# Attention, soft mixture of experts and a feed-forward layer in one kernel: the first slice of the folded feed-forward weight is made in two halves, six subtractions move from GpSimd to VectorE, and decode steps of ScalarE are placed behind the activations of their unit

## The chip, the cores and the metric

The kernel runs on one core of one Trainium2 chip. Its time is the device time of that core in microseconds (us). The engines work side by side, each through its own queue of instructions in order, and wait for one another through semaphores: TensorE (PE in the profile, with its weight loads as PEld), VectorE (DVE), ScalarE (ACT), GpSimd (POOL) and SyncE (SP), which only issues DMAs here.

## What is computed

```python
# attention: q, k, v (4, 8, 576, 64), window of 128, linear bias, softmax
scores = where(mask, q @ k.T / 8 + slope * -|i - j|, -1e9)
x = softmax(scores) @ v                        # -> (2304, 512)
# soft mixture of experts: 8 experts with 4 slots each
logits = x @ phi                               # (2304, 32)
slot_in = softmax(logits, axis=0).T @ x        # (32, 512)
slot_out[e] = relu(slot_in[e] @ w1[e]) @ w2[e] # (32, 512)
y = softmax(logits, axis=1) @ slot_out         # (2304, 512)
# feed-forward layer, d_ff = 2048
h = y @ w_in                                   # (2304, 2048)
out = maximum(0.01 * h, h) @ w_out             # (2304, 512)
```

`w_in` and `w_out` come as float64; the kernel reads each value as two 32-bit words and builds a float32 from them.

## The kernel before

The work runs in three stages: attention with the router's logits (to about 150 us), the experts (to about 210 us), and the feed-forward layer. The change lies in the last one.

**Folding.** `y @ w_in` is computed as `c @ (slot_out @ w_in)`, where `c` holds the combine weights. `M = slot_out @ w_in` has only 32 rows, so that the first layer is one matmul of 128 x 128 by 128 x 384 for each unit (`stage1`, L951). The operand of M is `mst`: its rows hold M's rounded high part and, on partitions 64 to 127, the remainder. `emit_M` (L918) makes M for one chunk or two of 256 columns in two parts. Part 0: four matmuls of `soT` (the slot outputs transposed) with the decoded `w_in` chunk, one for each 128 of the 512 rows, side by side on TensorE (L923), and a copy by ScalarE (L926). Part 1: a matmul with the constant `blk` that sums them (L928), a rounding copy by ScalarE into `mst` (L930), and a subtraction by VectorE that leaves the remainder (L931). `soT` comes from `to_soT` (L808): four transposes on TensorE and four copies by VectorE of 32 columns each (L814).

**Units.** The 2304 rows are taken in blocks of 384 (`TB`), the 2048 hidden columns in 16 groups of 128 (f). A unit is one block with one f; `visits` lists the 96 units in the order of work. For a unit, `stage1` puts the first layer into a PSUM tile `ph` (two buffers), `round_g` (ScalarE, L955) writes the activation rounded for TensorE, `full_g` (ScalarE, L959) the full one, `rest_g` (VectorE, L963) their difference, and `emit_o` (L965) adds nine matmuls of 512 columns (L973) into three PSUM accumulators: rounded activation by the rounded weight (WO1), by the weight's remainder (WO2), and remainder by the rounded weight. After the last f of a visit, `finish` moves the accumulators to a spill buffer, adds them to it, or writes the output; ScalarE does two of each three copies, VectorE one (L988).

**Decoding.** The weights come in eight chunks of `w_in` and eight of `w_out`, each 1 MB. `decode` (L733) turns one into float32 in two halves: a step on ScalarE for each half (`sq`, an Abs with a scale), three on VectorE (`ops`, a shift and two logical combinations), and for `w_out` a rounding copy by ScalarE into WO1 and a subtraction that leaves WO2 (`tail`, L771 and L772). All have line L757 in the profile. In chunk 0 the subtraction is VectorE's, in the others GpSimd's.

**The order** is a table of numbers: `at_(y, f)` enters a step at place y, in units, and the steps are issued sorted by y (L1057). `stage1` of unit n has y = n, its activations n + 0.121 and n + 0.174, its second layer n + 1.9 rising to n + 3.986. ScalarE's decode steps stand at y - 0.33 of their chunk's entry in `DEC`, M of later chunks at `MY`, and the transposes of the last batch of combine weights (`ctr`, L851) at 16.3 and 17.1. `keep` issues matmuls on constants that fill waits of TensorE; `WX` gives how many. SP issues the loads of later chunks in the order of `loads`.

Of the kernel before, what the change touches and what calls it, by code (L numbers as in the profile page):

```python
# [21 lines left out]
def attn_softmoe_ffn(ctx: ExitStack, tc: tile.TileContext, q, k, v, phi, w1, w2, w_in, w_out, cst_in, out):  # L22
    nc = tc.nc
# [96 lines left out]
    with tc.manual_schedule():  # L120
# [578 lines left out]
        FPC = NF // NCH  # L699
        fw = DFF // NCH  # L700
        TB = 384
        WX = {"i": 1, "s": 1, "t": 2, "m": 2, "b": 3, "h": 3}
        x0 = off["x0"]

        def parts(w, *os):
# [27 lines left out]
        def decode(c, split):  # L733
# [22 lines left out]
            def op(l, f, *a, **kw):  # L756
                l.append(lambda: f(*a, **kw))  # L757
# [9 lines left out]
            if split:  # L767
                for i, d in enumerate(dd):
                    w1v = WO1[c].rearrange("p a b -> p (a b)")[:, n * i:n * i + n]
                    w2v = WO2[c].rearrange("p a b -> p (a b)")[:, n * i:n * i + n]  # L770
                    op(tail, nc.scalar.copy, out=w1v, in_=d)  # L771
                    op(tail, (nc.gpsimd if c else nc.vector).tensor_tensor, out=w2v, in0=d, in1=w1v.bitcast(F32), op=ALU.subtract)  # L772
            return sq, ops, tail

        bctx = ExitStack()
# [142 lines left out]
        def emit_M(cs, part):  # L918
# [8 lines left out]
            else:  # L927
# [78 lines left out]
        def at_(y, f, *a):  # L1006
            ev.append((y, len(ev), lambda: f(*a)))

        for n, u in enumerate(units):
            o = n + min(1.9 + .13 * n, ZO["O"])  # L1010
            at_(n, stage1, *u)
            at_(n + ZO["T"], round_g, *u)
            at_(n + ZO["H"], full_g, *u)
            at_(n + ZO["V"], rest_g, *u)
            at_(o, emit_o, *u)
            if u[2] == visits[u[0]][3] - 1:
                for i in range(3):
# [89 lines left out]
```

## Time and profile before

| | |
|---|---|
| median of 3 runs | 451.87 us (450.97 to 452.1) |
| the profiled execution | 450.6 us, of which the span is 448.9 us |
| TensorE busy | 432.3 us (96%) |
| VectorE busy | 283.8 us (63%) |
| ScalarE busy | 240.7 us (54%) |
| GpSimd busy | 128.3 us (29%) |

The span runs from the first to the last instruction on the core; the profiled execution's own time has 1.7 us around it. It is 1.3 us below the median. The shares are means over stages with different limits, and a busy TensorE is not one at its peak, since its records overlap; so the stage in question is read from the timeline.

### The profile page before, as it was taken

How to read it: one execution, taken by the hardware profiler on the slowest of the kernel's cores; microseconds unless marked ns; L12 is line 12 of the kernel's file. 1: busy time of each engine (PE TensorE's matmuls, PEld its weight loads, DVE VectorE, ACT ScalarE, POOL GpSimd, SP SyncE). 2: the span in 40 equal slices, each digit the busy share in tenths (PEclk: the TensorE clock that was granted, in tenths of full speed). 3: DMA queues.
4: the chain of work that ended last, by engine and by line, in shares of the span. 5: the costliest groups of instructions: out<-in, count | busy, mean ns of one | idle time of the engine just before them, and what ended most of it. 6: DMA issues, size and time to landing. Idle time of an engine off the chain costs nothing.

```text
span 448.9 us, 9854 instructions
## 1 busy us (share of the span) xinstructions
PE 432.3 (96%) x3498; PEld 340.3 (76%) x3498; DVE 283.8 (63%) x887; ACT 240.7 (54%) x555; POOL 128.3 (29%) x302
## 2 busy tenths in 40 slices
PE   8899999999999999999998999999999999999996
PEld 7788888888888785334775788878878888888885
DVE  5999889999999945022798767675562223225242
ACT  4586777577677641021784865555545335333330
POOL 3477567576567743020010222020202000000000
PEclk9999999999999999999999999999999999999999
DMA  8389889889888878999966150000000003003011
GB/s 169 103 229 238 224 244 243 215 240 246 216 226 241 250 219 300 343 386 395 397 239 234 45 154 34 1 1 1 1 0 0 1 0 142 0 0 142 1 72 70
DMA packets 66834, 70.30 MB, mean 157 GB/s; under 512 B 23169, under 2 KB 42017, under 8 KB 66785
## 3 DMA queue, kind: packets, MB, share of 16 engines
q1 hardware_dynamic: 66640, 69.53, 50.7%
q8 instruction: 28, 0.46, 0.5%
q14 instruction: 22, 0.17, 0.1%
q10 hardware_dynamic: 144, 0.13, 0.1%
HBM read 64.85 MB, written 4.72 MB: 155 GB/s over the span
## 4 chain that ended last, share of the span: by engine, by line
PE 76%; DVE 9%; DMA 7%; ACT 5%; issue 2%; SPq 0%; POOL 0%; DVEq 0%; ACTq 0%; POOLq 0%
PE acc L973 41%; PE o_ps L407 4%; DMA qb<-ms 4%; PE ph L951 3%; PE pb L822 3%; PE st L343 3%; PE sm L301 3%; PE st L342 3%; DMA ar<-in_moe_w_out_dram 3%; PE tp L261 2%; PE o_ps L151 2%; DVE junk L311 2%; PE tp L449 1%; DVE kq L279 1%; PE pb L875 1%
## 5 line engine op out<-in xcount | busy, mean ns | idle before, releaser
L973 PE MATMUL acc<-p,p 128*128 128x512 f32 x648 | 161.1, 393 | 0.0
L973 PEld LDWEIGHTS acc<-p,p 128*128 128x128 f32 x648 | 120.4, 188 | 27.0 <-issue 2.6
L963 DVE TENSOR_TENSOR p<-ar,p 128x384 fp32r<-128x384 f32 x96 | 56.5, 598 | 98.2 <-ACT ar L959 98.1
L955 ACT ACTIVATE p<-ph 128x384 fp32r<-128x384 f32 x96 | 47.4, 493 | 96.2 <-PE ph L951 96.2
L973 PE MATMUL acc<-b,p 128*128 128x512 f32 x216 | 55.5, 400 | 1.3 <-DVE p L963 1.3
L311 DVE CUSTOM_DVE_ANT_0 junk<-sm,ar 128x256 bf16<-128x256 f32 (+2 forms) x160 | 53.5, 375 | 4.2 <-PE sm L301 4.0
L350 ACT ACTIVATE ar<-st 128x512 f32<-128x512 f32 x64 | 38.3, 599 | 19.3 <-PE st L343 10.2
L973 PEld LDWEIGHTS acc<-b,p 128*128 128x128 f32 x216 | 40.0, 188 | 10.8 <-DVE p L963 1.7
L959 ACT ACTIVATE ar<-ph 128x384 f32<-128x384 f32 x96 | 46.9, 488 | 0.0
L757 POOL TENSOR_TENSOR p<-ar,p 128x512 fp32r<-128x512 f32 x12 | 15.9, 1322 | 90.5 <-ACT p L757 58.8
L342 PE MATMUL st<-kq 128*128 128x256 f32 (+1 forms) x160 | 40.1, 278 | 0.0
L407 PE MATMUL o_ps<-ar 128*64 128x65 f32 x992 | 39.0, 225 | 0.0
L301 PE MATMUL sm<-kb,qb 96*128 96x256 f32 (+2 forms) x160 | 34.9, 312 | 3.4 <-ACT kb L274 1.4
L407 PEld LDWEIGHTS o_ps<-ar 128*64 128x64 f32 x992 | 34.8, 138 | 4.1 <-issue 1.5
L343 PE MATMUL st<-qb,kb 128*128 128x256 f32 (+1 forms) x160 | 36.2, 273 | 1.6 <-DMA qb<-ms 1.5
L951 PE MATMUL ph<-p,p 128*128 128x384 f32 x96 | 32.0, 338 | 0.7 <-DVE p L931 0.4
L274 ACT ACTIVATE qb<-tp 64x288 fp32r<-64x288 f32 x64 | 27.7, 433 | 9.1 <-PE tp L261 7.9
L279 DVE SCALAR_TENSOR_TENSOR kq<-tp,qb 64x288 fp32r<-64x288 f32 x64 | 29.2, 457 | 4.3 <-ACT qb L274 2.2
L287 POOL TENSOR_SCALAR_AFFINE_SELECT kq<-qb 64x576 fp32r<-64x576 f32 x32 | 21.1, 661 | 37.2 <-ACT qb L274 29.6
L274 ACT ACTIVATE kb<-tp 64x288 fp32r<-64x288 f32 x64 | 27.9, 437 | 6.0 <-PE tp L261 4.6
L343 PEld LDWEIGHTS st<-qb,kb 128*128 128x128 f32 (+1 forms) x160 | 28.6, 179 | 2.9 <-DMA qb<-ms 2.8
L281 DVE TENSOR_TENSOR kq<-tp,kb 64x288 fp32r<-64x288 f32 x64 | 29.1, 455 | 1.7
(190 smaller groups left out, 615.5 us busy)
## 6 DMA issues: line engine op xcount, KB each, us to landing
p<-in_moe_w_dram SPq DMA_DIRECT2D x56, 256.0 KB, 4.4
p<-in_moe_w_dram SPq DMA_DIRECT2D x7, 1024.0 KB, 11.6
p<-in_moe_w_in_dram SPq DMA_DIRECT2D x5, 1024.0 KB, 5.5
p<-in_moe_w_out_dram SPq DMA_DIRECT2D x5, 1024.0 KB, 15.4
ar<-in_k_dram SPq DMA_DIRECT2D x32, 144.0 KB, 4.0
ar<-in_q_dram SPq DMA_DIRECT2D x32, 144.0 KB, 3.7
out_dram<-ar SPq DMA_DIRECT2D x17, 256.0 KB, 2.2
ar<-in_v_dram SPq DMA_DIRECT2D x32, 128.0 KB, 3.9
```

Source lines behind the costliest of these rows:

```text
L274: nc.scalar.activation(out=b1, in_=pr, func=AF.Copy, scale=2.0 ** (g % H - 2) if half else 1.0)
L301: nc.tensor.matmul(sl, lhsT=Q1[0:MROW, 128 * t:128 * t + mr], rhs=K1[0:MROW, c0:c1], start=True, stop=True)
L311: nc.vector.tensor_tensor_reduce(out=jk[0:mr, 0:n], in0=sl, in1=maskt[0:mr, m0:m0 + n], op0=ALU.add, op1=ALU.max, accum_out=mn[g % 2][0:mr ...
L342: nc.tensor.matmul(sl, lhsT=KX[:, k0:k1], rhs=QA[:, q0:q1], start=True, stop=False)
L343: nc.tensor.matmul(sl, lhsT=kb[g % R][:, k0:k1], rhs=qb[g % R][:, q0:q1], start=False, stop=True)
L350: nc.scalar.activation(out=e, in_=sts.pop((g, s)), func=AF.Exp, scale=2.0 ** -(g % H + 1))
L407: nc.tensor.matmul(o_ps[64 * u:64 * u + 64, t, :], lhsT=lt, rhs=r, start=st, stop=sp, tile_position=(0, 64 * u))
L951: nc.tensor.matmul(p, lhsT=mst[:, 128 * f:128 * f + 128], rhs=rhs, start=True, stop=True)
L955: nc.scalar.activation(out=G[t0, f][0], in_=H1[t0, f], func=AF.Prelu, alpha=0.01)
L959: nc.scalar.activation(out=gg, in_=H1.pop((t0, f)), func=AF.Prelu, alpha=0.01)
L963: nc.vector.tensor_tensor(out=g2, in0=G0.pop((t0, f)), in1=g1.bitcast(F32), op=ALU.subtract)
L973: nc.tensor.matmul(acc[t0][t], lhsT=(g1, g1, g2)[k][:, 128 * t:128 * t + 128], rhs=(WO1, WO2, WO1)[k][c][:, i], start=(f == f0 and k == 0) ...
```

## The change

- `emit_M0` takes the place of `emit_M` for chunk 0. It makes M in two halves of 128 columns: both halves of part 0, then both of part 1, each with its own PSUM tile; the parts 1 use tiles of the accumulators (`acc3`, `acc4`).
- `to_soT` copies all 128 columns by one instruction of VectorE instead of four.
- ScalarE's first decode step of `w_out` chunk 0 stands ahead of M instead of behind its first copy.
- The rounded activation of unit 0 is made in two pieces, 128 and 256 columns.
- Three matmuls of `keep` fall away (`t`, `m` and `h`).
- The subtractions of `w_out` chunks 1 to 3, two each, are VectorE's instead of GpSimd's.
- ScalarE's decode steps stand at y - 0.25 instead of y - 0.33, so behind both activations of a unit instead of around the first; `finish` stands 0.02 later.
- M of chunks 2 and 3 stands at 12.05 instead of 12.2: part 0 is ahead of unit 9's second layer instead of behind it.
- The transposes of the last combine batch stand at 24.3 and 25.3 instead of 16.3 and 17.1, and with them the loads of `w_in` chunk 7 (into the slot that they read) and `w_out` chunk 7 at 26 instead of 14.65 and 20.15.

```diff
-        WX = {"i": 1, "s": 1, "t": 2, "m": 2, "b": 3, "h": 3}
+        WX = {"i": 1, "s": 1, "t": 1, "m": 1, "b": 3, "h": 2}
...
-                    op(tail, (nc.gpsimd if c else nc.vector).tensor_tensor, out=w2v, in0=d, in1=w1v.bitcast(F32), op=ALU.subtract)
+                    op(tail, (nc.gpsimd if c > 3 else nc.vector).tensor_tensor, out=w2v, in0=d, in1=w1v.bitcast(F32), op=ALU.subtract)
...
-            for j in range(4):
-                a, b2 = [t.rearrange("p k (g a) -> p k g a", g=2)[:, :, :, SPE * j:SPE * j + SPE] for t in (soT, p[:, :, 32 * j:32 * j + 32])]
-                nc.vector.tensor_copy(a, b2)
+            own = bass.AP(p.tensor, p.offset, [p.ap[0], [128, KD], [4 * SPE, 2], [32 + SPE, 4], [1, SPE]])
+            nc.vector.tensor_copy(soT.rearrange("p k (g j a) -> p k g j a", g=2, a=SPE), own)
...
+        def emit_M0(h, part):
+            sl = slice(128 * h, 128 * h + 128)
+            if part == 0:
+                p = psc.tile([128, 512], F32, tag="ph", name="ph")
+                for kc in range(KD):
+                    nc.tensor.matmul(p[32 * kc:32 * kc + 32, 0:128], lhsT=soT[:, kc, :], rhs=WI[0][0][:, kc, sl],
+                                     start=True, stop=True, tile_position=(0, 32 * kc))
+                if h == 0:
+                    M0["q"] = nxt("mq")
+                nc.scalar.copy(out=M0["q"][:, sl], in_=p[:, 0:128])
+            else:
+                p = psc.tile([128, 512], F32, tag=f"acc{3 + h}", name="acc", bufs=1)
+                nc.tensor.matmul(p[:, 0:128], lhsT=blk, rhs=M0["q"][:, sl], start=True, stop=True)
+                nc.scalar.copy(out=mst[:, sl], in_=p[:, 0:128])
+                nc.vector.tensor_tensor(out=mst[64:128, sl], in0=p[64:128, 0:128], in1=mst[64:128, sl].bitcast(F32), op=ALU.subtract)
...
-            nc.scalar.activation(out=G[t0, f][0], in_=H1[t0, f], func=AF.Prelu, alpha=0.01)
+            for c in (slice(0, TB),) if j or t0 or f else (slice(0, 128), slice(128, TB)):
+                nc.scalar.activation(out=G[t0, f][0][:, c], in_=H1[t0, f][:, c], func=AF.Prelu, alpha=0.01)
...
-        at_(-2, emit_M, (0,), 0)
+        for i in range(2):
+            at_(-2 + .01 * i, emit_M0, i, 0)
+            at_(-1 + .01 * i, emit_M0, i, 1)
...
-        MY = {1: 5.15, 3: 12.2, 5: 33.6, 7: 50.6}
+        MY = {1: 5.15, 3: 12.05, 5: 33.6, 7: 50.6}
...
-                at_(y - .33 + .01 * i, go, 0, i)
+                at_(y - .25 + .01 * i, go, 0, i)
...
-            at_(16.3 + .8 * i, lambda i: ctr(3, i, psc.tile([128, 512], F32, tag="ph", name="ph")), i)
+            at_(24.3 + i, lambda i: ctr(3, i, psc.tile([128, 512], F32, tag="ph", name="ph")), i)
```

**The start on TensorE**, from the transposes of `to_soT` to the second layer of unit 0. In the changed kernel L939 and L946 are the halves of M, L968 is `stage1`, L991 the second layer; `w` and the `acc<-ident` rows are `keep`. Before:

```order
L811 MATMUL pa<-ident,ar 128x128 x4
L792 MATMUL w<-ident 128x128 x2
L923 MATMUL ph<-ar 32x256 x4
L792 MATMUL acc<-ident 128x128 x2
L928 MATMUL ph<-ar,blk 128x256
L792 MATMUL acc<-ident 128x128 x3
L951 MATMUL ph<-p_3574,p_3723 128x384 x2
L792 MATMUL acc<-ident 128x128 x3
L973 MATMUL acc<-b_3642,p_3575 128x512 x3
```

Now:

```order
L811 MATMUL pa<-ident,ar 128x128 x4
L792 MATMUL w<-ident 128x128
L939 MATMUL ph<-ar 32x128 x8
L792 MATMUL acc<-ident 128x128
L946 MATMUL acc<-ar,blk 128x128 x2
L792 MATMUL acc<-ident 128x128 x3
L968 MATMUL ph<-p_3574,p_3719 128x384 x2
L792 MATMUL acc<-ident 128x128 x2
L991 MATMUL acc<-b_3642,p_3575 128x512 x3
```

Each step of M is two instructions of half the width, and unit 0's `stage1` needs only the first of each.

**ScalarE, units 2 to 4**, with the decode steps of `w_in` chunk 1 (the rows of 2x256). L955 and L959 are the two activations, now L973 and L977; `ph_3784` before and `ph_3789` now are unit 2. Before:

```order
L757 CAST b0_3642<-ar_71 128x512
L757 ACTIVATE ar_71<-ar_71 128x2x256
L955 ACTIVATE p10_3575<-ph_3784 128x384
L757 ACTIVATE ar_71<-ar_71 128x2x256
L959 ACTIVATE ar_71<-ph_3784 128x384
L955 ACTIVATE p10_3575<-ph_3797 128x384
L959 ACTIVATE ar_71<-ph_3797 128x384
L955 ACTIVATE p10_3575<-ph_3815 128x384
L988 COPY ql_73<-acc_3772 128x512
L959 ACTIVATE ar_71<-ph_3815 128x384
```

Now:

```order
L757 CAST b0_3642<-ar_71 128x512
L973 ACTIVATE p10_3575<-ph_3789 128x384
L977 ACTIVATE ar_71<-ph_3789 128x384
L757 ACTIVATE ar_71<-ar_71 128x2x256 x2
L973 ACTIVATE p10_3575<-ph_3802 128x384
L977 ACTIVATE ar_71<-ph_3802 128x384
L973 ACTIVATE p10_3575<-ph_3820 128x384
L977 ACTIVATE ar_71<-ph_3820 128x384
L1006 COPY ql_73<-acc_3777 128x512
```

Both decode steps stand behind unit 2's second activation, and the copies of `finish` behind unit 4's.

**VectorE, units 5 to 9**, with the decode of `w_in` chunks 2 (`b2`) and 3 (`p0`). L963, now L981, is the remainder of a unit's activation; L931, now L930, that of M of chunk 1. Before:

```order
L963 TENSOR_TENSOR p2_3724<-ar_71,p10_3575 128x384
L931 TENSOR_TENSOR p1_3723<-ph_3866,p1_3723 64x256
L963 TENSOR_TENSOR p2_3724<-ar_71,p10_3575 128x384
L757 TENSOR_SCALAR ar_71<-b2_3653 128x512 x2
L757 SCALAR_TENSOR_TENSOR ar_71<-b2_3653,ar_71 128x512 x2
L757 SCALAR_TENSOR_TENSOR ar_71<-ar_71 128x2x256 x2
L963 TENSOR_TENSOR p2_3724<-ar_71,p10_3575 128x384 x2
L757 TENSOR_SCALAR ar_71<-p0_3693 128x512 x2
L757 SCALAR_TENSOR_TENSOR ar_71<-p0_3693,ar_71 128x512 x2
L757 SCALAR_TENSOR_TENSOR ar_71<-ar_71 128x2x256 x2
```

Now:

```order
L930 TENSOR_TENSOR p1_3719<-ph_3871,p1_3719 64x256
L981 TENSOR_TENSOR p2_3720<-ar_71,p10_3575 128x384
L757 TENSOR_SCALAR ar_71<-b2_3653 128x512 x2
L757 SCALAR_TENSOR_TENSOR ar_71<-b2_3653,ar_71 128x512 x2
L757 SCALAR_TENSOR_TENSOR ar_71<-ar_71 128x2x256 x2
L981 TENSOR_TENSOR p2_3720<-ar_71,p10_3575 128x384
L757 TENSOR_TENSOR b1_3643<-ar_71,b0_3642 128x512
L981 TENSOR_TENSOR p2_3720<-ar_71,p10_3575 128x384
L757 TENSOR_SCALAR ar_71<-p0_3693 128x512 x2
L757 SCALAR_TENSOR_TENSOR ar_71<-p0_3693,ar_71 128x512 x2
L757 SCALAR_TENSOR_TENSOR ar_71<-ar_71 128x2x256
L757 TENSOR_TENSOR b1_3643<-ar_71,b0_3642 128x512
```

The two subtractions of `w_out` chunk 1 (`b1<-ar,b0`) are new in VectorE's queue, the first one behind the remainder of unit 7.

## Rows read from the trace of the kernel before

**Rows 1.** Busy us of each engine by stage; then granted clock, DMA share, GB/s.

```profile
core 0: us, PE busy (x) PEld busy (x) DVE busy (x) ACT busy (x) POOL busy (x), PEclk, DMA share, GB/s
209.80:215.00 5.20, 4.63 (x35) 3.50 (x35) 2.63 (x8) 3.05 (x7) 0.00 (x0) 1.00 1.03 395
215.00:240.00 25.00, 22.90 (x103) 17.34 (x104) 23.01 (x40) 18.34 (x41) 2.91 (x2) 1.00 0.80 299
264.00:436.00 172.00, 172.00 (x770) 140.21 (x769) 80.51 (x149) 81.53 (x180) 10.34 (x8) 1.00 0.08 30
```

**Rows 2.** TensorE's timeline, 266 to 274 us: start, length, instruction, [idle before <- releaser].

```profile
268.40 0.33 PE L951 MATMUL ph<-p,p 128*128 128x384 f32 x1
...
270.64 0.33 PE L951 MATMUL ph<-p,p 128*128 128x384 f32 x1
```

**Rows 3.** Timeline of all engines, 211 to 217 us.

```profile
211.48 0.48 DVE L814 COPY ar<-pa 128x32 f32<-128x32 f32 x4 [8.17 <-PE pa L811]
...
212.11 0.64 PE L923 MATMUL ph<-ar 128*32 128x256 f32 x8 [0.22 <-DVE ar L814]
...
212.85 0.37 ACT L926 COPY ar<-ph 128x256 f32<-128x256 f32 x1 [1.46 <-PE ph L923]
...
213.28 0.70 PE L928 MATMUL ph<-ar,blk 128*128 128x256 f32 x2
...
214.54 0.43 DVE L931 TENSOR_TENSOR p<-ph,p 64x256 fp32r<-64x256 f32 x1
...
215.03 0.62 PE L951 MATMUL ph<-p,p 128*128 128x384 f32 x2 [0.38 <-DVE p L931]
...
216.07 1.18 PE L973 MATMUL acc<-b,p 128*128 128x512 f32 x4
```

**Rows 4.** ScalarE's timeline, 219 to 221 us.

```profile
219.89 0.65 ACT L757 ACTIVATE ar<-ar 128x512 f32<-128x512 f32 x1
220.44 0.47 ACT L959 ACTIVATE ar<-ph 128x384 f32<-128x384 f32 x1
```

**Rows 5.** TensorE's timeline, 216 to 264 us.

```profile
220.96 0.44 PE L951 MATMUL ph<-p,p 128*128 128x384 f32 x1
...
224.12 1.14 PE L923 MATMUL ph<-ar 128*32 128x256 f32 x8 [0.45 <-ACT ar L959]
225.19 2.37 PE L973 MATMUL acc<-b,p 128*128 128x512 f32 x9
...
230.52 0.45 PE L951 MATMUL ph<-p,p 128*128 128x384 f32 x1 [0.25 <-ACT ar L959]
...
237.25 1.90 PE L973 MATMUL acc<-b,p 128*128 128x512 f32 x7 [1.28 <-DVE p L963]
...
245.58 1.12 PE L928 MATMUL ph<-ar,blk 128*128 128x512 f32 x2 [0.33 <-ACT ar L926]
...
254.16 0.66 PE L855 MATMUL ph<-ident,p 128*128 128x128 f32 x4 [0.64 <-ACT ar L959]
...
263.92 0.33 PE L951 MATMUL ph<-p,p 128*128 128x384 f32 x1
```

**Rows 6.** VectorE's timeline, 231 to 242 us.

```profile
232.02 2.40 DVE L757 SCALAR_TENSOR_TENSOR ar<-b,ar 128x512 int32<-128x512 int32 x2
234.35 1.28 DVE L757 SCALAR_TENSOR_TENSOR ar<-ar 128x512 int32<-128x512 int32 x2
235.55 2.12 DVE L963 TENSOR_TENSOR p<-ar,p 128x384 fp32r<-128x384 f32 x2
...
240.67 1.01 DVE L963 TENSOR_TENSOR p<-ar,p 128x384 fp32r<-128x384 f32 x2
```

**Rows 7.** GpSimd's timeline, 230 to 264 us.

```profile
232.46 1.42 POOL L757 TENSOR_TENSOR b<-ar,b 128x512 fp32r<-128x512 f32 x1 [32.87 <-ACT b L757]
235.29 1.50 POOL L757 TENSOR_TENSOR b<-ar,b 128x512 fp32r<-128x512 f32 x1 [1.42 <-ACT b L757]
```

**Rows 8.** Groups by line, 209 to 264 us: busy us, mean ns, idle before.

```profile
L757 DVE TENSOR_TENSOR b<-ar,b 128x512 fp32r<-128x512 f32 x2 | 1.4, 692 | 0.4 <-ACT b L757 0.4
```

**Rows 9.** The page's DMA issues: count, size of each, median us to landing.

```profile
p<-in_moe_w_out_dram SPq DMA_DIRECT2D x5, 1024.0 KB, 15.4
```

More of the change, by code (lines that the diff above doesn't have):

```diff
@@ L808, in to_soT @@
         def to_soT():
-            p = ps.tile([128, 4, 128], F32, tag="pa", name="pa")
+            p = ps.tile([128, 4, 128], F32, tag="pa", name="pa")[:, :, :]
             for kc in range(KD):
                 nc.tensor.transpose(p[:, kc, :], so[:, 128 * kc:128 * kc + 128], ident)
-            for j in range(4):
-                a, b2 = [t.rearrange("p k (g a) -> p k g a", g=2)[:, :, :, SPE * j:SPE * j + SPE] for t in (soT, p[:, :, 32 * j:32 * j + 32])]
-                nc.vector.tensor_copy(a, b2)
+            own = bass.AP(p.tensor, p.offset, [p.ap[0], [128, KD], [4 * SPE, 2], [32 + SPE, 4], [1, SPE]])
+            nc.vector.tensor_copy(soT.rearrange("p k (g j a) -> p k g j a", g=2, a=SPE), own)
         for h in range(2):
@@ L931, in emit_M @@
                 nc.vector.tensor_tensor(out=mst[64:128, sl], in0=p[64:128, 0:n], in1=mst[64:128, sl].bitcast(F32), op=ALU.subtract)
+        M0 = {}
+        def emit_M0(h, part):
[13 more added lines that the diff above has]
+                nc.vector.tensor_tensor(out=mst[64:128, sl], in0=p[64:128, 0:128], in1=mst[64:128, sl].bitcast(F32), op=ALU.subtract)
         visits = [(0, 768, 0, 2), (768, 768, 0, 4), (0, 768, 2, 8), (768, 768, 4, 8), (1536, 768, 0, NF),
@@ L1017, in attn_softmoe_ffn @@
                 for i in range(3):
-                    at_(o + (i if u[0] == NV - 2 else .01 * i), finish)
-        at_(-2, emit_M, (0,), 0)
+                    at_(o + (i if u[0] == NV - 2 else .02 + .01 * i), finish)
+        for i in range(2):
+            at_(-2 + .01 * i, emit_M0, i, 0)
+            at_(-1 + .01 * i, emit_M0, i, 1)
         at_(-1.9, keep, WX["m"], wpc)
-        at_(-1 + ZO["M1"], emit_M, (0,), 1)
         at_(-.9, keep, WX["b"], wpc)
@@ L1024, in attn_softmoe_ffn @@
         loads = [(load_wi, 4, "p9"), (load_wo, 4, "a3"), (load_wi, 5, "a2"), (load_wo, 5, "b2"), (load_wi, 6, "p13"),
-                 (load_wo, 6, "p0"), (load_wi, 7, "p12"), (load_wo, 7, "p9")]
+                 (load_wo, 6, "p0")]
+        at_(26, load_wi, 7, "p12")
+        at_(26.1, load_wo, 7, "p9")
         DEC = {1: (2.45, 4.65), 2: (6.45, 10.95), 3: (8.45, 13.95), 4: (19.45, 22.45), 5: (28.45, 31.45), 6: (37.45, 40.45), 7: (45.45, 48.45)}
-        MY = {1: 5.15, 3: 12.2, 5: 33.6, 7: 50.6}
+        MY = {1: 5.15, 3: 12.05, 5: 33.6, 7: 50.6}
         def dec(c, split, y):
@@ L1043, in attn_softmoe_ffn @@
         at_(1.5, *loads.pop(0))
-        for y, k, i in ((-1.8, 0, 0), (-1.75, 1, 0), (-1.74, 1, 2), (-1.5, 1, 4), (-.95, 2, 0), (-.9, 2, 1), (-.8, 1, 1),
+        for y, k, i in ((-2.1, 0, 0), (-1.75, 1, 0), (-1.74, 1, 2), (-1.5, 1, 4), (-.95, 2, 0), (-.9, 2, 1), (-.8, 1, 1),
                         (.22, 0, 1), (.4, 1, 3), (.45, 1, 5), (1.25, 2, 2), (1.4, 2, 3)):
```

## The prediction

> **What bounds the kernel now.** I read the busy time by stage first, then TensorE's timeline where its rows stand apart, then the engine that each late row names. From 264 to 436 us TensorE is busy 172.00 of 172.00 us [rows 1], and one unit (a first-layer matmul and nine second-layer ones) follows another in 2.24 us: 268.40 to 270.64 [rows 2]. Nothing that ScalarE, VectorE or GpSimd do there can change the end. What can be had lies ahead of 264 us: in 209.8 to 215 us a chain runs through four engines, and from 215 to 240 us VectorE is busy 23.01 of 25 us [rows 1] while TensorE shows waits. TensorE is fully loaded behind this, so each microsecond by which the first-layer matmul of unit 20, now at 263.92 [rows 5], comes earlier is a microsecond of the end, less what work is moved behind it.
>
> How much is there? Units 0 to 20 stand between 215.03 [rows 3] and 263.92, 48.9 us. Their own work: 17 emit groups at 2.24 are 38.1; three more first-layer matmuls at 0.17; M of chunks 2 and 3 is 2.0 (the window of 172.0 us holds 75 units, 168.0 us, and two such M), M of chunk 1 half of that; the transposes of the last combine batch 0.7. Together 42.3, so 6.6 us are waits. That caps the gain of this stretch.
>
> **The change part by part**, as starts on TensorE, before and worked out.
>
> *M in halves, the one copy, the split activation.* The chain now [rows 3]: four copies 211.48 to 211.96 (0.48), matmul 212.11 (0.64), copy on ScalarE 212.85 (0.37), matmul 213.28 (0.70), the same copy again, subtraction on VectorE 214.54 (0.43), unit 0 at 215.03; its second layer starts 1.04 later, at 216.07, when the first activation is done. Of this only the first half of M has to pass now. One copy of 128 columns lies between a quarter of 0.48 and 0.48; VectorE takes 0.43 for 256 columns and 0.69 for 512 [rows 3, 8], 1.0 ns a column, so I take 0.30. A matmul step of 128 columns lies between half and all of the 256-column one; I take 0.43 for 0.64 and 0.48 for 0.70. ScalarE takes 0.65 for 512 columns [rows 4] and 0.37 for 256, so 0.25 for 128. The subtraction is 0.30 by VectorE's slope. With the gaps between the steps as now: 211.48 + 0.30 + 0.15 + 0.43 + 0.10 + 0.25 + 0.06 + 0.48 + 0.03 + 0.25 + 0.04 + 0.30 + 0.06 = 213.93, against 215.03. Activating the first 128 columns alone saves another 0.2 of the 1.04. **Term: -1.3.** If a half costs as much as the whole, 0.4 is left; if exactly half, 1.9. The second half follows 0.3 behind on each engine and is first read by unit 2, some 3 us later, which covers it. The three dummy matmuls fewer cost nothing: they fill waits, and the granted clock is 1.00 also from 215 to 240 us [rows 1], with waits of over 1 us.
>
> [...]
>
> *Decode steps behind the activations.* Now a decode step of 0.65 stands between the two activations of unit 2, whose second one ends at 220.91 [rows 4]; TensorE's unit 4 waits for that at 220.96 [rows 5]. With the pair behind them the wait is gone, and unit 4 comes at 219.5: **-0.2** beyond the start's 1.3. VectorE's remainder of unit 2 comes at 218.7 (220.9 less 1.3, less two steps at 0.55, and 0.2 for the order on ScalarE). The decode of chunk 1 ends 3.7 behind it, as now, at 222.4, and with it the wait of M of chunk 1 (224.12): the second layer of unit 3 moves from 225.19 [rows 5] to 223.0, **-0.7** more. Unit 7 at 230.52 waits for the second activation of unit 6, again behind a decode step; without that it is at 227.9, **-0.4** more. What is late next is VectorE.
>
> *Low parts on VectorE.* GpSimd takes 1.42 and 1.50 for the first two of its six subtractions [rows 7], VectorE 0.69 for one [rows 8]. While GpSimd subtracts, VectorE's instructions stretch: a pair of decode steps takes 2.40 where the next pair takes 1.28, and two remainders 2.12 where two take 1.01 later [rows 6]. So in this stretch VectorE gives 2 x 0.60 (half of 1.28 is the spacing, a little less) and gets 1.1 + 1.1 back. The remainder of unit 7 now lets TensorE go on at 237.25 after a wait [rows 5]. From VectorE's remainder of unit 2 to that of unit 7 are 14.6 us now (220.9, where unit 2's activation ends, to 235.55), 13.5 without the stretched pair: 218.7 + 13.5 + 0.56 = 232.8. TensorE comes to the matmul that reads it at 227.9 + 2 x 2.24 + 0.6 = 233.0. The wait is gone: **-1.6** more, with 0.2 to spare. If this cover fails, VectorE's lateness is TensorE's one for one. Behind unit 8 VectorE is ahead by over 1 us.
>
> [...]
>
> *M of chunks 2 and 3 ahead of unit 9's second layer.* It now takes the PSUM tile of unit 11, started 0.17 before, and waits for both its activations, 1.2 behind that start: about 0.75 of idle TensorE. In return its second part no longer waits for the copy of the first (0.33 at 245.58, and gaps around it [rows 5]). **+0.1**, between -0.6 and +1.3 (if ScalarE still has a decode pair of 1.2 ahead).
>
> *Transposes of the last batch behind unit 24.* Now they wait 0.64 at 254.16 for a PSUM tile whose reader stands behind copies [rows 5]; with the gaps around it (0.36) and their own work (0.7) they delay units 17 to 20 by 1.7. Behind unit 24 ScalarE has nothing queued, so the waits go and 0.7 of work comes back later: **-1.0**. The load into the slot that they read is moved behind them on SP's queue, with the one after it; both chunks are needed some 20 units later, 44 us, against a median of 15.4 to land [rows 9]. No other DMA moves. DMA runs at 395 GB/s ahead of 215 us and at 299 up to 240 [rows 1]; no row of TensorE's waits names it.
>
> **Sum.** 1.3 + 0.2 + 0.7 + 0.4 + 1.6 - 0.1 + 1.0 = 5.1. A schedule by hand hides small slips; I take 0.4 back. -4.7 against the profiled execution's 450.6 gives 445.9. That execution is 1.3 below the median of the runs, 451.87, so the forecast for a median is **447.2**. Its own range, by the bounds above, is 445.9 to 448.4.
>
> **The rivals.**
> *VectorE stays the bound.* If the rows were stretched by something other than GpSimd, the subtractions only lengthen VectorE's queue, by 1.2 ahead of unit 8, and the wait now at 237.25 stays: the gain there is 1.5, what the start gives, and 1.0 from the transposes: 449.4. For it: VectorE hardly idles in that stretch. Against: the stretching falls on GpSimd's spans. [...] 0.13.
> *The early M costs more.* TensorE stands behind unit 11's activations while ScalarE is still in the decode pair: 0.75 + 1.2, so 448.4. 0.08.
> *The change doesn't do what it says.* If loads and not engines end these waits, an earlier start only waits longer: 451.9. Against it: the waits name ScalarE and VectorE. 0.05.
> *Slower: VectorE stands behind ScalarE's rounding copy.* Each of the four subtractions of chunks 2 and 3 waits in VectorE's queue for a copy that ScalarE issues behind the next unit's first activation; behind it stands the copy that frees an accumulator for unit 13. By my times this is free at 249.75 and wanted at 249.9; from that point on each wait is TensorE's. With a unit's cadence less the subtraction (2.24 - 0.60) lost at each of the four, 6.6 go and 4.7 come: 453.8. Against: GpSimd waited for the same copies, and ScalarE's queue gets shorter ahead of them. 0.04.
>
> **How the numbers follow.** The forecast has 0.70. It and the first two rivals lie in 445.9 to 449.6, 0.91 less the tails of each. About 0.3% (1.4 us) is what a measurement of this kernel can tell from no change: faster is these three, 0.91; same 0.05; slower 0.04.
>
> **What would show it.** Right: unit 0 near 213.9 and its second layer near 214.8; no stretched remainder on VectorE and no GpSimd subtraction ahead of 264 us; no wait at unit 7's second layer; a wait of 0.5 to 1 for M of chunks 2 and 3; transposes without a wait behind unit 24; unit 20 near 258; 2.24 a unit afterwards. Wrong: remainders of 1 us with GpSimd idle, TensorE waiting for VectorE between units 8 and 16, or unit 20 behind 260.5.

## The result, and the profile after

The changed kernel takes **447.12 us** (median of 4 runs, 446.24 to 447.83) against 451.99 for the kernel before (4 runs, 450.97 to 452.43): ratio 0.989, 95% interval 0.985 to 0.9931. Forecast were 447.2 and "faster". The profiled execution takes 446.24 us with a span of 444.5, 4.4 less than before; the prediction's sum was 4.7.

The stages first, as in [rows 1]:

```profile
215.00:240.00 25.00, 24.18 (x114) 18.19 (x113) 24.51 (x48) 20.21 (x45) 0.00 (x0) 1.00 0.93 343
264.00:436.00 172.00, 172.00 (x770) 139.97 (x770) 77.70 (x141) 80.99 (x181) 10.34 (x8) 1.00 0.10 36
```

TensorE, the first column behind the length, is busy 24.18 of 25 us where it was 22.90, GpSimd (the fifth) has nothing left there, and the full stage behind is as full as it was. VectorE (the third) rose from 23.01 to 24.51: more work is done in the same 25 us, and it hardly idles.

The start, all engines, answering to [rows 3]. This execution's experts end 0.17 us later (its first `keep` is at 209.90, that of before at 209.73).

```profile
211.66 0.29 DVE L813 COPY ar<-pa 128x128 f32<-128x128 f32 x1 [8.17 <-PE pa L811]
...
212.09 0.64 PE L939 MATMUL ph<-ar 128*32 128x128 f32 x16 [0.25 <-DVE ar L813]
...
212.62 0.44 ACT L943 COPY ar<-ph 128x128 f32<-128x128 f32 x2 [0.50 <-PE ph L939]
...
212.99 0.66 PE L946 MATMUL acc<-ar,blk 128*128 128x128 f32 x4
...
213.46 0.49 ACT L947 CAST p<-acc 128x128 fp32r<-128x128 f32 x2 [0.40 <-PE acc L946]
...
213.83 0.50 DVE L948 TENSOR_TENSOR p<-acc,p 64x128 fp32r<-64x128 f32 x2
...
214.18 0.62 PE L968 MATMUL ph<-p,p 128*128 128x384 f32 x2
...
215.00 2.39 PE L991 MATMUL acc<-b,p 128*128 128x512 f32 x9
```

Each step still does the whole M (x16, x2, x4), but the next one begins when the first half is there: ScalarE's copy at 212.62 starts 0.11 before TensorE's row ends, and TensorE's second step at 212.99 before ScalarE's pair ends at 213.06. Unit 0 is at 214.18, its second layer at 215.00.

TensorE after that, answering to [rows 5]:

```profile
219.67 0.34 PE L968 MATMUL ph<-p,p 128*128 128x384 f32 x1
...
223.38 2.36 PE L991 MATMUL acc<-b,p 128*128 128x512 f32 x9
...
228.29 0.34 PE L968 MATMUL ph<-p,p 128*128 128x384 f32 x1
...
233.02 2.25 PE L991 MATMUL acc<-b,p 128*128 128x512 f32 x9
...
238.69 1.06 PE L922 MATMUL ph<-ar 128*32 128x512 f32 x8 [0.79 <-ACT ar L977]
...
258.70 0.33 PE L968 MATMUL ph<-p,p 128*128 128x384 f32 x1
...
267.83 0.60 PE L854 MATMUL ph<-ident,p 128*128 128x128 f32 x4
...
270.61 0.27 PE L854 MATMUL ph<-ident,p 64*128 64x64 f32 x1
```

Units 4 and 7 (219.67, 228.29) and unit 3's second layer (223.38) start without a wait. Unit 7's second layer runs its nine matmuls in one piece from 233.02. One wait is left, the 0.79 that the early M brings. Unit 20 is at 258.70, where it was at 263.92. The transposes stand at 267.83 and 270.61 without a wait.

VectorE, answering to [rows 6]:

```profile
230.21 1.28 DVE L757 SCALAR_TENSOR_TENSOR ar<-b,ar 128x512 int32<-128x512 int32 x2
231.41 1.28 DVE L757 SCALAR_TENSOR_TENSOR ar<-ar 128x512 int32<-128x512 int32 x2
232.61 0.55 DVE L981 TENSOR_TENSOR p<-ar,p 128x384 fp32r<-128x384 f32 x1
233.08 0.68 DVE L757 TENSOR_TENSOR b<-ar,b 128x512 fp32r<-128x512 f32 x1
...
249.69 0.68 DVE L1006 COPY qx<-acc 128x512 f32<-128x512 f32 x1
```

The pair that took 2.40 takes 1.28, the remainder of unit 7 (232.61) one share of 0.55, and the first moved subtraction stands right behind it. The last row is the accumulator copy on which the rival "slower" rested. It starts at 249.69 and ends at 250.37; the forecast had the accumulator free at 249.75. TensorE first writes there with the fourth matmul of unit 13's second layer:

```profile
249.74 2.35 PE L991 MATMUL acc<-b,p 128*128 128x512 f32 x9
```

By the trace's single instructions this fourth matmul starts at 250.43, 0.06 after the copy's end, and the row is 0.1 longer than the 2.25 of its neighbours. So the copy was late against the forecast, but TensorE's need for it was late by about as much.

**A measure for parts.** Nothing ahead of the feed-forward stage changes in any kernel here, yet the first `keep` behind the experts lies between 209.15 and 212.25 us in the profiled executions. So parts are compared by the time on TensorE from that matmul on, in the profiled executions (to the first-layer matmul of a unit, and to the end of the last matmul). The medians are of all runs of a kernel. In some runs the mean granted clock is 0.996 or less and the time mostly longer (8 of R1's ten runs, 7 of R7's ten, none of the changed kernel's four), so a microsecond between two medians is read from the stage instead, and R3's ratio leaves out its slowest run. The kernel before had 451.69, 451.36 and 451.63 beside R1 to R3 and R8, R4 to R6 and R10, R7 and R9. The last three rows are versions tried for a gain.

| kernel | unit 0 | 4 | 7 | 10 | 14 | 20 | end | median of runs |
|---|---|---|---|---|---|---|---|---|
| before | 5.30 | 11.23 | 20.79 | 29.26 | 38.91 | 54.19 | 235.11 | 451.99 |
| changed | 4.28 | 9.77 | 18.39 | 25.21 | 35.11 | 48.80 | 230.59 | 447.12 |
| changed, subtractions back (R1) | 4.28 | 9.79 | 18.40 | 27.27 | 37.16 | 50.80 | 232.58 | 450.07 |
| changed, old decode places (R2) | 4.29 | 10.37 | 19.91 | 26.83 | 36.73 | 50.42 | 232.21 | 449.58 |
| changed, M whole (R3) | 4.98 | 10.49 | 19.01 | 25.83 | 35.73 | 49.39 | 231.18 | 448.07 |
| changed, transposes back (R4) | 4.28 | 9.77 | 18.41 | 25.23 | 35.13 | 50.44 | 231.36 | 447.42 |
| changed, M of 2 and 3 back (R5) | 4.28 | 9.78 | 18.38 | 25.20 | 35.20 | 48.89 | 230.67 | 447.17 |
| before, subtractions moved (R6) | 5.30 | 11.23 | 20.78 | 27.71 | 37.37 | 52.69 | 233.61 | 449.35 |
| before, decode places moved (R7) | 5.30 | 10.98 | 19.27 | 28.12 | 37.77 | 53.06 | 233.98 | 451.88 |
| both M steps shifted (R8) | 4.29 | 9.78 | 18.68 | 25.50 | 34.20 | 48.89 | 230.67 | 447.62 |
| R8 and chunk 3 decoded later (R9) | 4.28 | 9.78 | 18.67 | 25.49 | 34.20 | 48.19 | 229.98 | 446.13 |
| R9 with M of chunk 1 apart (R10) | 4.28 | 9.78 | 17.61 | 25.06 | 34.21 | 48.20 | 229.98 | 445.48 |

The changed kernel ends 4.52 us sooner in this measure.

### The profile page after: what moved, and what is told of

Its sections match the earlier page's. It is cut to its first block, busy times and chain, and to the rows that moved or that the text cites. A ratio compares the mean times of both kernels' runs of the same rounds, so it can differ in the third digit from the quotient of the medians.

```text
span 444.5 us, 9878 instructions
## 1 busy us (share of the span) xinstructions
PE 429.8 (97%) x3502; PEld 339.5 (76%) x3502; DVE 283.0 (64%) x891; ACT 240.7 (54%) x558; POOL 119.9 (27%) x296
## 4 chain that ended last, share of the span: by engine, by line
PE 84%; DVE 6%; ACT 3%; DMA 3%; issue 2%; POOL 1%; SPq 0%; DVEq 0%; ACTq 0%; POOLq 0%
PE acc L991 45%; PE o_ps L407 5%; PE ph L968 4%; PE sm L301 4%; PE pb L821 3%; PE pb L874 3%; PE st L343 3%; PE st L342 3%; DMA qb<-ms 3%; PE tp L261 2%; PE o_ps L151 2%; DVE junk L311 1%; PE tp L449 1%; DVE kq L281 1%; DVE kq L279 1%
## 5 line engine op out<-in xcount | busy, mean ns | idle before, releaser
L991 PE MATMUL acc<-p,p 128*128 128x512 f32 x648 | 161.3, 394 | 0.0
L991 PEld LDWEIGHTS acc<-p,p 128*128 128x128 f32 x648 | 120.4, 188 | 26.9 <-issue 2.6
L981 DVE TENSOR_TENSOR p<-ar,p 128x384 fp32r<-128x384 f32 x96 | 53.2, 556 | 93.7 <-ACT ar L977 93.6
L973 ACT ACTIVATE p<-ph 128x384 fp32r<-128x384 f32 (+1 forms) x97 | 47.6, 492 | 95.0 <-PE ph L968 94.9
L991 PE MATMUL acc<-b,p 128*128 128x512 f32 x216 | 54.9, 398 | 0.0
L991 PEld LDWEIGHTS acc<-b,p 128*128 128x128 f32 x216 | 40.0, 188 | 10.2 <-issue 1.5
L977 ACT ACTIVATE ar<-ph 128x384 f32<-128x384 f32 x96 | 47.0, 490 | 0.0
L757 POOL TENSOR_TENSOR p<-ar,p 128x512 fp32r<-128x512 f32 x8 | 10.3, 1293 | 128.7 <-ACT p L757 110.5
L968 PE MATMUL ph<-p,p 128*128 128x384 f32 x96 | 32.1, 340 | 0.0
```

Source lines behind the costliest of these rows:

```text
L968: nc.tensor.matmul(p, lhsT=mst[:, 128 * f:128 * f + 128], rhs=rhs, start=True, stop=True)
L973: nc.scalar.activation(out=G[t0, f][0][:, c], in_=H1[t0, f][:, c], func=AF.Prelu, alpha=0.01)
L977: nc.scalar.activation(out=gg, in_=H1.pop((t0, f)), func=AF.Prelu, alpha=0.01)
L981: nc.vector.tensor_tensor(out=g2, in0=G0.pop((t0, f)), in1=g1.bitcast(F32), op=ALU.subtract)
L991: nc.tensor.matmul(acc[t0][t], lhsT=(g1, g1, g2)[k][:, 128 * t:128 * t + 128], rhs=(WO1, WO2, WO1)[k][c][:, i], start=(f == f0 and k == 0) ...
```

## Experiments

### The subtractions, both ways (R1, R6)

In the changed kernel they go back to GpSimd:

```diff
-op(tail, (nc.gpsimd if c > 3 else nc.vector).tensor_tensor, ...)
+op(tail, (nc.gpsimd if c else nc.vector).tensor_tensor, ...)
```

> The changed kernel with the six subtractions of w_out chunks 1 to 3 back on GpSimd, the rest as changed. Theory (a subtraction of GpSimd stretches the VectorE instructions that read two SBUF operands beside it): the pair of decode steps ahead of unit 7's remainder takes about 2.4 us again instead of 1.28, the remainders of units 7 and 8 about 1 us each, and TensorE waits at unit 7's second layer for 0.8 to 2.5 us, where the changed kernel has no wait; the VectorE wait of 0.81 for ScalarE's rounding copy at 247 us is gone, but nothing waits for it. Time 1 to 2.5 us above the changed kernel, so 448.1 to 449.6. [...]

Measured: 450.07 us (448.63 to 452.26), ratio to before 0.9969 (0.9943 to 0.9995). The total lies 0.5 above what was expected; the stage is 1.99 longer, inside the 1 to 2.5. Until unit 9 nothing differs; then all 2.0 us go between units 9 and 10. VectorE:

```profile
231.80 2.40 DVE L757 SCALAR_TENSOR_TENSOR ar<-b,ar 128x512 int32<-128x512 int32 x2
234.12 1.28 DVE L757 SCALAR_TENSOR_TENSOR ar<-ar 128x512 int32<-128x512 int32 x2
235.33 2.11 DVE L981 TENSOR_TENSOR p<-ar,p 128x384 fp32r<-128x384 f32 x2
```

and GpSimd and TensorE:

```profile
231.72 1.33 POOL L757 TENSOR_TENSOR b<-ar,b 128x512 fp32r<-128x512 f32 x1 [30.37 <-ACT b L757]
235.12 1.43 POOL L757 TENSOR_TENSOR b<-ar,b 128x512 fp32r<-128x512 f32 x1 [2.07 <-ACT b L757]
```

```profile
237.02 1.90 PE L991 MATMUL acc<-b,p 128*128 128x512 f32 x7 [1.79 <-DVE p L981]
```

The two VectorE rows that are long start within 0.25 us of GpSimd's two; the pair between them, from 234.12, has its 1.28. Unit 7's second layer pays with a wait of 1.79.

The other way round, the move alone in the kernel before:

```diff
-op(tail, (nc.gpsimd if c else nc.vector).tensor_tensor, ...)
+op(tail, (nc.gpsimd if c > 3 else nc.vector).tensor_tensor, ...)
```

> The kernel before with only the six subtractions of low parts of chunks 1 to 3 moved from GpSimd to VectorE. Theory (the move is worth what it was in the changed kernel, 2.0 us, where that stood in the bound): the pairs of scalar_tensor_tensor of 2.40 us shrink to about 1.28, the remainders of 2.12 for two to about 1.0, the wait of TensorE on VectorE at unit 7's second layer (1.28 us) falls under 0.3, and unit 10 comes 1.0 to 2.0 us sooner than in the kernel before; some of it may be taken back at waits on ScalarE that stand behind. Total 450.0 to 451.0. [...]

Measured: 449.35 us (448.76 to 451.7), ratio 0.9962 (0.9938 to 0.9986). The pair and the remainder on VectorE:

```profile
232.35 1.29 DVE L757 SCALAR_TENSOR_TENSOR ar<-b,ar 128x512 int32<-128x512 int32 x2
...
234.75 0.55 DVE L963 TENSOR_TENSOR p<-ar,p 128x384 fp32r<-128x384 f32 x1
```

TensorE:

```profile
235.68 2.26 PE L973 MATMUL acc<-b,p 128*128 128x512 f32 x9
```

No wait is left at unit 7's second layer (this row), unit 10 comes 1.55 sooner, and 1.50 of it reaches the end. The total fell by more than was expected (449.35, against 450.0 to 451.0); by the trace the stage gives 1.50 of these 2.0. The view that the move gains nothing falls in both directions: the stage changes by 1.99 and by 1.50.

### The places of the decode steps, both ways (R2, R7)

```diff
-                at_(y - .25 + .01 * i, go, 0, i)
+                at_(y - .33 + .01 * i, go, 0, i)
...
-                    at_(o + (i if u[0] == NV - 2 else .02 + .01 * i), finish)
+                    at_(o + (i if u[0] == NV - 2 else .01 * i), finish)
```

> The changed kernel with ScalarE's decode steps back at y - 0.33 and the copies of finish back at their old places. Theory (each decode step between two activations delays the PSUM tile's release by 0.55 us, and VectorE's chain that starts with unit 2's remainder by as much): a wait of 0.2 to 0.4 us at unit 4, M of chunk 1 later by 0.7, a wait at unit 7 of 0.3 to 0.7; 1.0 to 1.8 us above the changed kernel, 448.1 to 448.9. Rival (ScalarE has the room anyway, the order is hidden behind TensorE's nine matmuls): within 0.4 us, 446.7 to 447.5.

Measured: 449.58 us (447.32 to 453.82), ratio 0.9959 (0.9922 to 0.9995), the stage 1.62 longer. TensorE:

```profile
220.72 0.44 PE L968 MATMUL ph<-p,p 128*128 128x384 f32 x1 [0.43 <-ACT ar L977]
...
223.88 1.14 PE L922 MATMUL ph<-ar 128*32 128x256 f32 x8 [0.46 <-ACT ar L977]
...
230.26 0.45 PE L968 MATMUL ph<-p,p 128*128 128x384 f32 x1 [0.25 <-ACT ar L977]
```

Waits on ScalarE stand again at unit 4, at M of chunk 1 and at unit 7, the three places of the prediction [rows 5], and unit 7 comes 1.52 later. The sizes were less exact: 0.43 at unit 4 (expected 0.2 to 0.4), 0.25 at unit 7 (0.3 to 0.7), and M of chunk 1 comes 1.12 later, not 0.7. The stage is within the 1.0 to 1.8 expected, the total 0.7 above its range.

The same edit the other way in the kernel before:

> The kernel before with only the decode steps of ScalarE and the copies that end a visit moved behind the activations of their unit (the three places that the prediction put at 0.2, 0.7 and 0.4 us). Theory: unit 7 comes 1.2 to 1.6 us sooner than in the kernel before, as it came 1.52 later when this part alone was undone; of that a part is taken back at unit 7's second layer, which waits for VectorE's stretched pair there, so unit 10 and the end of the stage come only 0.4 to 1.2 us sooner, total 450.2 to 451.0, and the wait on VectorE grows from 1.28 to over 1.8. This is why the parts undone one by one add up to more than the whole. Rival: the pair stands later as well, since its own input comes from ScalarE, the wait stays at 1.28 and the end comes 1.2 to 1.6 sooner (449.8 to 450.2).

Measured: 451.88 us (449.64 to 454.72), ratio 1.0003 (0.9974 to 1.0031). The total misses what was expected: it shows no gain, though the profiled execution took 449.64 us. In the profiled execution unit 7 comes 1.52 sooner, and TensorE's wait behind it grows from 1.28 to 1.77 (a little under the 1.8 expected), on the stretched pair that stands on VectorE as before:

```profile
236.31 1.90 PE L973 MATMUL acc<-b,p 128*128 128x512 f32 x7 [1.77 <-DVE p L963]
```

```profile
231.10 2.40 DVE L757 SCALAR_TENSOR_TENSOR ar<-b,ar 128x512 int32<-128x512 int32 x2
```

The stage ends 1.13 sooner. So in the profiled execution the theory holds. The parts undone one at a time (1.99 + 1.62 + 0.59 + 0.77 + 0.08 = 5.05 us) add up to more than the 4.52 of all, and one reason is shown here: with one of the two waits left in place, it swallows a part of what the other edit gains. Each of the two is worth 0.49 less alone (1.50 and 1.13) than beside the other (1.99 and 1.62). That is not the whole of it, since 0.54 of the start's gain (see R3) was never undone and is not in the 5.05; what swallows the rest wasn't tested.

### M of chunk 0 whole (R3)

```diff
-        for i in range(2):
-            at_(-2 + .01 * i, emit_M0, i, 0)
-            at_(-1 + .01 * i, emit_M0, i, 1)
+        at_(-2, emit_M, (0,), 0)
+        at_(-1 + ZO["M1"], emit_M, (0,), 1)
```

> The changed kernel with M of chunk 0 whole again (the single copy into soT, the split activation and the fewer dummy matmuls stay). Theory (the halves shorten each of five steps by 0.12 to 0.22 us): unit 0 comes 0.75 to 0.95 us later after the experts' last matmul than in the changed kernel, and the end by as much: 447.8 to 448.1. [...]

Measured: 448.07 us (446.4 to 453.58), ratio 0.9915 (0.9887 to 0.9943). TensorE:

```profile
212.17 0.64 PE L922 MATMUL ph<-ar 128*32 128x256 f32 x8 [0.25 <-DVE ar L813]
...
213.34 0.70 PE L927 MATMUL ph<-ar,blk 128*128 128x256 f32 x2
...
214.96 0.62 PE L968 MATMUL ph<-p,p 128*128 128x384 f32 x2 [0.26 <-DVE p L930]
```

Unit 0 comes 0.70 later and the end 0.59: the halves are worth that, a little less than the 0.75 to 0.95 expected. The other 0.32 by which unit 0 moved (4.98 against 5.30) comes with the single copy, ScalarE's earlier decode step and the `keep` that fell away, and another 0.22 from unit 0 to its second layer (0.82 instead of 1.04) stays here beside the split activation. These were not taken apart.

### The transposes back (R4)

```diff
-            at_(24.3 + i, lambda i: ctr(3, i, ...), i)
+            at_(16.3 + .8 * i, lambda i: ctr(3, i, ...), i)
```

> The changed kernel with only the two sets of four transposes back at their old places, behind the first layers of units 16 and 17. Theory (the term of 1.0 us): there the second set waits for a PSUM buffer that ScalarE's activations still hold, so the time from the first small matmul after the experts to unit 20 becomes longer by 0.6 to 1.1 us more than the 0.9 that merely moves (the transposes lie before unit 20 again), and the end of the stage comes 0.3 to 1.1 us later than in the changed kernel; the trace shows a TensorE wait on ScalarE of 0.3 us or more at or just behind the transposes. Total 447.4 to 448.3. Rival: without the stretched decode ahead of them ScalarE is in time, the transposes cost the same 0.9 in either place, the end moves by less than 0.2 and no wait shows.

Measured: 447.42 us (446.51 to 450.04), ratio 0.9916 (0.9891 to 0.994). The wait is back, as in [rows 5]:

```profile
251.03 0.63 PE L854 MATMUL ph<-ident,p 128*128 128x128 f32 x4 [0.71 <-ACT ar L977]
```

The theory held: unit 20 comes 1.64 later and the end 0.77; 0.87 is the transposes' own time on TensorE, which the changed kernel pays at units 24 and 25 instead.

### M of chunks 2 and 3, and what stands behind it (R5, R8, R9, R10)

First this step alone at its old place:

```diff
-        MY = {1: 5.15, 3: 12.05, 5: 33.6, 7: 50.6}
+        MY = {1: 5.15, 3: 12.2, 5: 33.6, 7: 50.6}
```

> The changed kernel with only the block sums of chunks 2 and 3 back at their old place, behind the first layer of unit 12. Theory: the wait of 0.79 us ahead of the eight matmuls goes (they stand 2 units behind ScalarE's activation that frees the buffer), but the second set waits for ScalarE's copy again by 0.3 to 0.6, and what is left of the gain, 0.1 to 0.5, is taken back where the second layers wait for VectorE's copy of an accumulator, as when both block sums were moved: end of the stage within 0.25 of the changed kernel. Total 446.6 to 447.6. Rival: the early place is a plain loss of 0.8 that comes out whole: 446.2 to 446.5, stage shorter by 0.6 to 0.9. Other rival: the early place was needed, the wait of 0.33 with its idle TensorE costs more: stage longer by 0.3 or more.

Measured: 447.17 us (445.9 to 448.67), ratio 0.9903 (0.9872 to 0.9934), the stage within 0.08. The wait of 0.79 goes, and the second part waits for ScalarE's copy of the first again; by unit 14 the time that was won is lost (35.20 against 35.11):

```profile
244.40 1.13 PE L927 MATMUL ph<-ar,blk 128*128 128x512 f32 x2 [0.33 <-ACT ar L925]
```

So the first theory held in the end of the stage and in this wait: the two places are worth the same, by two different waits. Its last step isn't seen: up to unit 14 no wait on VectorE of 0.2 us or more shows, and from there to unit 17 both kernels take the same 6.92. A place without either, and the same for chunk 1:

```diff
-                    at_(MY[c] + .9 * i, emit_M, cs, i)
+                    at_(MY[c] + (1.1 if c == 3 else .9) * i, emit_M, cs, i)
...
-        MY = {1: 5.15, 3: 12.05, 5: 33.6, 7: 50.6}
+        MY = {1: 5.35, 3: 12.2, 5: 33.6, 7: 50.6}
```

> The changed kernel with M of chunk 1 behind unit 3's second layer (5.35 instead of 5.15) and M of chunks 2 and 3 behind unit 9's second layer with its second part behind unit 10's (12.2 and 13.3 instead of 12.05 and 12.95). Theory (TensorE is now stopped at two places, by the decode of chunk 1 for some 0.75 us at 222 us and by unit 11's activations for 0.79 us at 238 us; placed later, both waits are covered by second-layer work): both gone, 1.2 to 1.5 us below the changed kernel, 445.6 to 445.9. Rival (the waits are covered by VectorE's lateness: remove them, and TensorE waits for remainders instead): less than 0.4 us, 446.7 to 447.1, with VectorE named at waits between units 3 and 12.

Measured: 447.62 us (446.0 to 448.5), ratio 0.9894 (0.9847 to 0.9942). No gain: the theory fell. The rival held in that waits named by other engines take the gain back, but not in their places: one is on ScalarE, at the second part of M of chunk 1, and the one on VectorE comes at unit 13's second layer, behind the units that it named; the total lies above its range too. TensorE:

```profile
225.62 0.70 PE L927 MATMUL ph<-ar,blk 128*128 128x256 f32 x2 [0.61 <-ACT ar L925]
...
250.15 1.67 PE L991 MATMUL acc<-b,p 128*128 128x512 f32 x6 [0.39 <-DVE qx L1006]
```

and VectorE:

```profile
248.08 0.68 DVE L757 SCALAR_TENSOR_TENSOR ar<-p,ar 128x512 int32<-128x512 int32 x1
248.69 0.68 DVE L757 SCALAR_TENSOR_TENSOR ar<-ar 128x512 int32<-128x512 int32 x1
249.40 0.69 DVE L1006 COPY qx<-acc 128x512 f32<-128x512 f32 x1
```

Unit 14 comes 0.91 sooner than in the changed kernel, and by unit 17 that is gone (42.07 against 42.03): TensorE now waits for VectorE's accumulator copy, which stands behind a subtraction and decode steps. This is the place, though not the size, of the prediction's rival "slower". If that copy is the bound, putting it ahead of the decode must give the 0.8 back:

```diff
-        DEC = {..., 3: (8.45, 13.95), ...}
+        DEC = {..., 3: (8.45, 14.45), ...}
```

> The kernel with both block sums moved (which ended where the changed kernel did), with one thing more: the decode of w_out chunk 3 half a unit later, so that VectorE's copy of unit 11's accumulator stands ahead of its four scalar_tensor_tensor. Theory: the 0.8 us won by unit 14 was taken back by that copy, which came at 249.40 where the second layer behind it was ready to go on at 249.76; now it starts 2.4 us sooner at about 247.0, the wait of 0.39 us goes, unit 17 and unit 20 come 0.5 to 0.8 us sooner than in that kernel, total 446.2 to 446.7. Rival: the wait goes but another takes its place before unit 20 (VectorE has no gap there), gain under 0.2, total 446.9 to 447.5.

Measured: 446.13 us (445.82 to 446.96), ratio 0.9873 (0.9851 to 0.9895). VectorE:

```profile
248.58 0.69 DVE L1006 COPY qx<-acc 128x512 f32<-128x512 f32 x1
...
250.33 1.29 DVE L757 SCALAR_TENSOR_TENSOR ar<-p,ar 128x512 int32<-128x512 int32 x2
```

This execution's experts end 1.66 us later than R8's, so the copy stands 2.48 sooner within the stage; the wait is gone, unit 20 comes 0.70 sooner, and so does the end (0.69). The theory held. R10, made before R9, has the second part of M of chunk 1 at 6.5, behind the second layer of unit 4, besides:

> The changed kernel with three shifts: block sums of chunk 1 at 5.35 and 6.5 units (the second set behind the second layer of unit 4), block sums of chunks 2 and 3 at 12.2 and 13.3, and the decode of w_out chunk 3 by half a unit later, so that VectorE's copy of unit 11's accumulator stands ahead of its four scalar_tensor_tensor. Theory: what took back the gain when both block sums were moved was (a) the wait of 0.61 us at the second set of chunk 1 and (b) the wait of 0.39 us for that copy; with both gone unit 7 comes 0.3 to 0.7 us and unit 20 0.8 to 1.5 us sooner than in the changed kernel, total 445.6 to 446.4. Rival: a next wait lies close behind these (VectorE is busy without a gap there), the gain at unit 20 is under 0.3 and the total 446.9 to 447.5.

Measured: **445.48 us** (444.42 to 447.23), ratio 0.987 (0.9831 to 0.9909), the fastest here. In the stage it ends where R9 does: unit 20 comes 0.60 sooner than in the changed kernel, less than the 0.8 expected and more than the rival's 0.3. Unit 7 comes 0.78 sooner than in the changed kernel and unit 10 only 0.15: a wait for VectorE takes it back in between.

```profile
237.70 1.90 PE L991 MATMUL acc<-b,p 128*128 128x512 f32 x7 [0.23 <-DVE p L981]
```

So the gain over the changed kernel that the trace shows, 0.61 us, is there in R9 already, with M of chunks 2 and 3 in a place with no wait and the copy ahead of the decode. Shifting the second part of chunk 1 adds nothing that the stage shows, and the intervals of the two totals overlap. No run has the other two shifts with M of chunk 1 left at its old place, so what its first shift is worth stays open.

## Why the prediction was right

Its steps against the trace, as gains in the measure of the table, each beyond the ones ahead of it (unit 3's and unit 0's second layers from their rows in the same way):

| step | forecast | measured |
|---|---|---|
| M in halves, to unit 0's second layer | 1.3 | 1.24 |
| decode order, unit 4 | 0.2 | 0.22 |
| decode order, unit 3's second layer | 0.7 | 0.52 |
| decode order, unit 7 | 0.4 | 0.42 |
| low parts on VectorE, unit 10 | 1.6 | 1.65 |
| M of 2 and 3 early, unit 14 | -0.1 | -0.25 |
| transposes, units 14 to 20 | 1.7 | 1.59 |
| transposes, behind unit 20 | -0.7 | -0.87 |
| sum | 5.1, less 0.4 taken back | 4.52 |

The rows are differences along the way to unit 20, not what each part is worth by itself: undone alone, the early M of chunks 2 and 3 costs nothing (R5, 0.08), the decode places are worth 1.62 and the subtractions 1.99.

No step failed in its mechanism, and R1 to R4 show the four large terms each by itself. The four slips of 0.1 to 0.2 (unit 3's second layer, the early M, and the transposes on both sides) all lie on the same side and add up to 0.6, where 0.4 had been taken back for slips. That the median came within 0.1 us of the forecast is in part luck. The profiled execution took 446.24, 0.3 above the 445.9 worked out for it, and the median lies 0.9 above that execution where 1.3 had been added: two misses that cancel.

*The start.* The price of a half was the uncertain number. The row of 128 columns on ScalarE is 0.44 for two where one of 256 took 0.37 [rows 3], the rounding copy's 0.49 where one took 0.37, VectorE's 0.50 for two where one took 0.43. So the fixed share is small in these rows, as the prediction took it. The halved copies read PSUM; no run here halves one that reads SBUF. In this chain of dependent steps 0.07 to 0.12 us more work in each of these pairs bought 0.70 us at unit 0 (R3).

*Low parts on VectorE.* This was the term with 0.2 to spare. The remainder of unit 7 ended at 233.16 (forecast 232.8, in an execution 0.17 later), and the matmul that reads it stands about 0.6 behind 233.02. R1 and R6 show that the move and nothing else takes the stretch away. The move is worth 1.5 us by itself and 2.0 with the rest, as GpSimd's row of 1.33 lengthened VectorE's by 1.12 (R1), while VectorE does the same subtraction in 0.68. What in the two engines makes their rows lengthen together, no trace here shows.

*The rivals.* "VectorE stays the bound" would have shown long rows on VectorE with GpSimd idle: there are none. "The early M costs more" would have shown 1.2 us beside the 0.75: the wait is 0.79. "The change doesn't do what it says" would have left the waits in place and 451.9: they went. "Slower" had the right place. The copy was free at 250.37, not 249.75, but it was wanted at 250.43, not 249.9, so in the changed kernel it was just in time and cost at most 0.1. R8 shows what stands behind it, some 0.7 us and not 6.6: one wait at one copy, not one at each of the four subtractions.

## What to carry to other kernels

A chain across engines that starts a full stage can be shortened by handing on halves, if the rows show that two halves together cost little more than the whole (here 0.44 against 0.37 on ScalarE, for 0.70 us at unit 0); read the price from rows of two widths of the same operation. Where two engines' rows lengthen together, the slower one's operation can be worth more on the other engine than it costs there (here a subtraction of 0.68 on VectorE for 1.12 of lengthening). When an edit wins time at one place and the end doesn't move, look for the next queue behind: what R8 lost there came back in R9, when one copy was put ahead of decode work that was not urgent.

## What was not expected of the hardware

In these traces, what GpSimd's subtraction does to VectorE depends on what VectorE reads: beside it a copy out of PSUM kept its 0.68, and a remainder of 0.55 took 1.05. The kernel before shows both kinds beside one GpSimd row. GpSimd:

```profile
251.54 1.51 POOL L757 TENSOR_TENSOR p<-ar,p 128x512 fp32r<-128x512 f32 x1 [14.76 <-ACT p L757]
```

VectorE:

```profile
251.82 0.68 DVE L988 COPY qx<-acc 128x512 f32<-128x512 f32 x1
252.42 1.05 DVE L963 TENSOR_TENSOR p<-ar,p 128x384 fp32r<-128x384 f32 x1
```

The copy out of a PSUM accumulator, wholly inside GpSimd's span, has its usual 0.68; the remainder behind it, with two operands that are not in PSUM, takes 1.05 for a usual 0.55. So beside this row not the whole engine is slowed but certain instructions. The stretched rows quoted here all have two such operands; which other forms are hit was not tried.

It also depends on which of the two starts first: a decode step that started 0.32 ahead kept its 0.68, a remainder that started 0.35 behind took 1.36. In the same trace, VectorE and GpSimd:

```profile
251.22 0.68 DVE L757 SCALAR_TENSOR_TENSOR ar<-ar 128x512 int32<-128x512 int32 x1
...
258.52 1.29 POOL L757 TENSOR_TENSOR p<-ar,p 128x512 fp32r<-128x512 f32 x1 [3.31 <-ACT p L757]
258.87 1.36 DVE L963 TENSOR_TENSOR p<-ar,p 128x384 fp32r<-128x384 f32 x1 [2.77 <-ACT ar L959]
```

The decode step at 251.22, both of whose operands are in SBUF too (where the kernel's tiles outside PSUM lie), started 0.32 before GpSimd's 251.54 and has its usual 0.68, though its last 0.36 lie beside it. The two remainders started behind GpSimd's row, one 0.88 and one 0.35, and both end 0.42 after it does (253.47 against 253.05, 260.23 against 259.81), whether that makes 1.05 or 1.36. So in these rows the remainder isn't slowed by a factor: it ends 0.42 after the subtraction that it found running. The pair of 2.40 [rows 6] is alike: in the trace its second instruction alone takes 1.80, its first, which started ahead of GpSimd's, 0.68. The second ends 0.54 after GpSimd's row.
